# Attention, MoE and gated MoE on one core: batches 1 to 3 of the first MoE as four blocks of 432 tokens, single q and k rows, one ring of three decode tiles

## The chip, the core and the metric

The kernel runs on 1 core of a Trainium2 chip. The time is that of the device in microseconds (us). Before the change it is 1085.62 us, the median of 3 runs (1084.67 to 1086.32). One further execution was profiled; all rows below are from it.

## The reference, cut to what matters

```python
# q, k, v: 4 batches, 8 heads, 576 tokens, 64 wide
local = softmax(causal(q @ k.T / 8)) @ v
mem   = (phi(q) @ M_prev) / (phi(q) @ z_prev + 1e-6)     # phi(x) = elu(x) + 1
attn  = g * mem + (1 - g) * local                        # g = sigmoid(beta), one per head
x = attn as [2304 tokens, 512]
h = x @ w_in                 # 512 -> 2048    the first MoE
x = (h * sigmoid(h)) @ w_out # 2048 -> 512
g, val = x @ w_gate, x @ w_val   # 512 -> 1536   the second MoE
out = (g * sigmoid(g) * val) @ w_out2            # 1536 -> 512
```

All weights and inputs come as 64-bit floats. q, k and v are read as they are handed over to the kernel in 32 bits; the MoE weights arrive as 64-bit words, and the kernel decodes them to 32 bits on chip.

## The kernel before

A matmul of the MoEs is done in three passes of fp32r, as a 32-bit number is split into a high part (rounded to fp32r) and a low part: high times high, low weight times high x, high weight times low x. That is why a product over 512 inputs (4 tiles of 128) takes 12 matmuls.

Attention is done in units. A unit is a batch and a pair of heads (128 rows). Batch 0 has two units for a pair: phase A for its first 256 tokens, phase B for the other 320. Batches 1 to 3 (phase G) have one unit for all 576. A unit loads rows of q, k and v, transposes q and k on TensorE (L340), makes the scores (L407, L482), their exponentials on ScalarE, scales them (L496 on GpSimd, L500 on ScalarE), transposes them, multiplies by v (`AV`, L592), and `put_x` (L306) writes the result, 128 of the 512 inputs of the MoE, as a high part (ScalarE, L314) and a low part (VectorE, L315). The four pairs of a batch together fill its x. Rows of q, k and v stand in two sets of tiles used in turn (`rows`, L228); `nxt_load` (L604) loads the rows of the unit after the next, q and k in the stage `lq`, v in `lv`.

The first MoE (`moe1`, L799) is a list of segments. A segment is a block of tokens and a slice of 512 of the 2048 hidden numbers: 4 hidden tiles of 12 matmuls each (`s1`, L829: "h"), and then 4 output tiles of 12 matmuls each (L888: "y"), 96 matmuls in all. For each hidden tile ScalarE makes the tanh (L836), VectorE the product (L837), ScalarE the high part gh (L838), and GpSimd the low part gl (L839). Output tiles are added up over the slices in yp (L891 on ScalarE for the first slice, L893 on VectorE), and written to DRAM after the last. Each batch has two blocks, of 256 and of 320 tokens, hence 8 segments a batch, 32 in all. The first two hidden tiles of a segment are issued before the output tiles of the one before (`la`). A slice needs 8 tiles of split weights of 512 KB; they are decoded and split once, written to DRAM, and read back (w<-wd, L733) whenever the slice comes again.

The second MoE's weights are decoded and split beside all this by `prep_w2` (L930): 36 tiles, each loaded as raw 64-bit words (L690, L695; the load waits for a one-column copy on GpSimd, L688), decoded by one ScalarE instruction (L704) and three on VectorE (L705 to L707) into a tile t from a ring of 4, combined in sums on GpSimd (L976 to L979, L1002 to L1005), split (high on ScalarE, low on GpSimd, L956), and written to DRAM (L941). It is advanced by one step after every third group of 12 matmuls while attention goes on (`every`), and after every third group once attention is done (`late`, L1068). After the last segment the second MoE runs on TensorE in an order written out by hand (L1164, L1271).

How far attention is at each segment is set by `goals` (L1369 on): a batch's attention is to be done when the cost (matmul columns) of the segments before its first one has been issued, less a share. A scheduler then settles the order on each engine by its own model of time, and SyncE issues all these DMAs in one queue, in order.

## Time and profile before

| | us |
|---|---|
| median of 3 runs | 1085.62 |
| the profiled execution's own time | 1084.78 |
| its span, first to last instruction | 1083.0 |
| TensorE busy in matmuls | 1048.6 (97%) |
| VectorE, ScalarE, GpSimd busy | 704.4, 547.7, 405.6 |
| last "y" of the first MoE ends at | 679.4 |

A row of a window gives, for a stretch of the span, the busy time of each engine and in brackets its number of instructions. A row of the timeline gives the start, the time to the end of the last of its instructions, the engine, the line, the operation, the tiles and "x" with the count. Matmuls of one row overlap, so the spacing of matmuls is read from the starts of two rows, not from the duration of one.

### The profile page before, as it was taken

The page shows a single profiled execution, that of the slowest core. Times are in us where ns is not written, and L with a number is a line of the kernel's source. Part 1 is how long each engine was busy: PE and PEld are TensorE (multiplying, and loading weights), DVE is VectorE, ACT ScalarE, POOL GpSimd, SP SyncE. Part 2 cuts the span into 40 slices and gives each one's busy share as a digit, 9 for nine tenths or more (in the row PEclk, how much of TensorE's full clock was granted, in tenths as well). Part 3 has the DMA queues.
Part 4 walks back from the last instruction along what each step waited for, and adds up shares of the span by engine and source line. Part 5 has one row for each costly group of instructions (what it writes and reads, how often), then busy time and mean ns, then how long its engine had stood idle before and what let it go on. Part 6 is the DMA issues. An engine that isn't in the chain of part 4 may idle for free.

```text
span 1083.0 us, 20683 instructions
## 1 busy us (share of the span) xinstructions
PE 1048.6 (97%) x7390; PEld 977.9 (90%) x7390; DVE 704.4 (65%) x1633; ACT 547.7 (51%) x1319; POOL 405.6 (37%) x493
## 2 busy tenths in 40 slices
PE   7788999999999999999999999999999999999998
PEld 5566888888999898989889999999999999999998
DVE  7897588987566665456766654465854569355573
ACT  6655586766557565646655543233622336232351
POOL 4577445568566563757543985000000000000000
PEclk9889999999999999999999999999999999999999
DMA  7968576566688664975628899777887778877784
GB/s 180 299 206 259 144 245 198 171 189 208 207 263 252 207 191 128 313 258 187 209 69 303 318 365 311 258 251 247 329 293 231 262 253 277 280 241 247 258 278 151
DMA packets 169831, 258.29 MB, mean 238 GB/s; under 512 B 76928, under 2 KB 114304, under 8 KB 169728
## 3 DMA queue, kind: packets, MB, share of 16 engines
q1 hardware_dynamic: 168640, 256.70, 71.8%
q8 instruction: 59, 0.97, 0.4%
q10 hardware_dynamic: 1088, 0.26, 0.1%
q14 instruction: 44, 0.36, 0.1%
HBM read 197.67 MB, written 59.24 MB: 237 GB/s over the span
## 4 chain that ended last, share of the span: by engine, by line
PE 76%; DVE 8%; DMA 7%; POOL 4%; issue 2%; ACT 1%; SPq 1%; POOLq 0%; DVEq 0%; ACTq 0%
PE h L829 14%; PE y L888 13%; PE oac L1164 10%; PE gb L1164 10%; PE po L1271 9%; PE pb L1271 4%; PE gd L1164 3%; PE U L592 3%; PE pst L340 3%; PE pss L407 3%; DMA raw<-in_moe_w_gate_dram 2%; DMA raw<-in_moe_w_val_dram 1%; PE psm L418 1%; PE pss L482 1%; POOL s L496 1%
## 5 line engine op out<-in xcount | busy, mean ns | idle before, releaser
L888 PE MATMUL y<-gh,w 128*128 128x320 f32 (+1 forms) x1024 | 172.8, 305 | 3.7 <-DVE yp L893 1.3
L829 PE MATMUL h<-xh,w 128*128 128x320 f32 (+1 forms) x1024 | 171.8, 305 | 4.2 <-DVE th L837 2.0
L829 PEld LDWEIGHTS h<-xh,w 128*128 128x128 f32 x1024 | 145.3, 190 | 13.7 <-issue 5.0
L888 PEld LDWEIGHTS y<-gh,w 128*128 128x128 f32 x1024 | 146.2, 190 | 9.2 <-DVE th L837 2.1
L839 POOL TENSOR_TENSOR gl<-th,gh 128x256 fp32r<-128x256 f32 (+1 forms) x128 | 113.1, 886 | 99.3 <-ACT gh L213 83.8
L1164 PE MATMUL gb<-yT,w 128*128 128x384 f32 x648 | 124.8, 336 | 0.0
L1164 PEld LDWEIGHTS gb<-yT,w 128*128 128x128 f32 x648 | 113.1, 188 | 0.0
L837 DVE SCALAR_TENSOR_TENSOR th<-th,h 128x256 f32<-128x256 f32 (+1 forms) x128 | 57.3, 449 | 73.8 <-ACT th L836 73.7
L888 PE MATMUL y<-gl,w 128*128 128x320 f32 (+1 forms) x512 | 94.4, 300 | 0.1
L1271 PE MATMUL po<-w,ph 128*128 128x256 f32 x516 | 93.8, 283 | 0.0
L829 PE MATMUL h<-xl,w 128*128 128x320 f32 (+1 forms) x512 | 91.8, 299 | 0.0
L496 POOL TENSOR_TENSOR s<-s,r 128x128 f32<-128x128 f32 (+4 forms) x96 | 72.5, 781 | 48.5 <-DVE r L508 14.0
L463 ACT ACTIVATE s<-s,mn 128x128 f32<-128x128 f32 (+3 forms) x128 | 71.0, 556 | 35.8 <-DVE mn L459 34.5
L1164 PE MATMUL oac<-yB,w 128*128 128x384 f32 x432 | 81.3, 336 | 0.0
L1271 PEld LDWEIGHTS po<-w,ph 128*128 128x128 f32 x516 | 81.2, 191 | 0.0
L1236 ACT CAST ph<-r 128x384 fp32r<-128x384 f32 x108 | 51.0, 513 | 55.7 <-DVE r L1190 35.7
L213 ACT CAST gh<-th 128x256 fp32r<-128x256 f32 (+1 forms) x128 | 55.0, 432 | 45.5 <-DVE th L837 39.6
L888 PEld LDWEIGHTS y<-gl,w 128*128 128x128 f32 x512 | 76.7, 190 | 1.2 <-issue 0.7
L829 PEld LDWEIGHTS h<-xl,w 128*128 128x128 f32 x512 | 75.9, 190 | 0.9 <-issue 0.4
L1164 PEld LDWEIGHTS oac<-yB,w 128*128 128x128 f32 x432 | 75.4, 188 | 0.0
L1271 PE MATMUL po<-w,pl 128*128 128x256 f32 x258 | 73.0, 283 | 0.0
L340 PE MATMUL pst<-ident,s 128*128 128x128 f32 x400 | 60.7, 279 | 10.2 <-POOL s L496 4.7
(166 smaller groups left out, 2152.2 us busy)
## 6 DMA issues: line engine op xcount, KB each, us to landing
w<-wg SPq DMA_DIRECT2D x108, 512.0 KB, 4.7
w<-wd SPq DMA_DIRECT2D x80, 512.0 KB, 5.5
wg<-wo SPq DMA_DIRECT2D x36, 512.0 KB, 3.5
w<-woT SPq DMA_DIRECT2D x36, 512.0 KB, 4.9
wd<-w SPq DMA_DIRECT2D x32, 512.0 KB, 3.3
raw<-in_moe_w_out_dram SPq DMA_DIRECT2D x28, 512.0 KB, 5.7
w<-woB SPq DMA_DIRECT2D x27, 512.0 KB, 4.7
w<-wg SPq DMA_DIRECT2D x36, 256.0 KB, 4.8
```

Source lines behind the costliest of these rows:

```text
L213: nc.scalar.copy(out, in_)
L340: nc.tensor.matmul(dst, src, ident[0:n, 0:n], start=start, stop=True, is_transpose=True, skip_group_check=True)
L407: lambda m=m, qx=qx, kx=kx, hh=hh, r=slice(64 * hh, 64 * hh + 64): nc.tensor.matmul(dst(hh), o[qx][r, x:x + P], o[kx][r, 0:w], start=(m == ...
L463: nc.scalar.activation(out=a, in_=a, func=ACTF.Exp, scale=-1.0, bias=mn, accum_out=o["sm", sup][:, col:col + 1])
L496: nc.gpsimd.tensor_mul(a, a, r.to_broadcast([P, w]))
L829: nc.tensor.matmul(ps[:, :nt], w[:, kk, :], x[:, kk, :nt], start=(m == 0), stop=(m == 3 * KD - 1))
L837: nc.vector.scalar_tensor_tensor(th[:, :nt], th[:, :nt], 1.0, ps[:, :nt], ALU.add, ALU.mult)
L839: tt(CFG["gl" if n >= CFG["n0"] else "gl0"]).tensor_sub(gl[:, :nt], th[:, :nt], f(gh[:, :nt]))
L888: nc.tensor.matmul(ps[:, :nt], w[:, c], g[:, :nt], start=(m == 0), stop=(m == last))
L1164: nc.tensor.matmul(dst, w[wi][:, P * kk:P * kk + P], y[ny][:, yi, kk], start=(start and m == 0), stop=(stop and m == 5), skip_group_check= ...
L1236: nc.scalar.copy(ph, src)
L1271: nc.tensor.matmul(dst, a[:, c], x, start=(begin and m == 0 and own_bank), stop=(end and m == 2), skip_group_check=True,)
```

## The change

Batch 0 keeps its blocks of 256 and 320. The 1728 tokens of batches 1 to 3 become four blocks of 432 (called t0 to t3 here), which run across the borders of batches: t0 holds tokens of batch 1 only, t1 of batches 1 and 2, t2 of 2 and 3, t3 of 3. t0 goes through its four slices alone, then t1 alone, then t2 and t3 together slice by slice. So the first MoE has 8 + 16 = 24 segments. `put_x` writes a unit's tokens into one or two blocks. x and yp get new homes: x of batch 0 and then of t2 in one tile, those of t0 and t3 in another, that of t1 in a third, which is later yp of t3.

q and k rows exist once; the rows for the next unit (no longer the one after it) are loaded in `lq`, after this unit's transposes. v keeps two tiles.

`decode` takes its tile from one ring of three for the weights of both MoEs; before, the first MoE's weights had a ring of 2 and those of the second one of 4.

`late` becomes 0.75: once attention is done, `prep_w2` is advanced after three of four groups of matmuls.

```diff
-    raw=2,
-    yp=2,
+    raw=3,
...
-    late=3,
+    late=0.75,
...
-    TM = SB
+    TB = 432
+    NB1 = (B - 1) * S // TB
+    TM = max(SB, TB)
...
-            t = {nm: ld.tile([P, 5, 2, D], F32, name=f"{nm}_t{i}") for nm in "qkv"}
+            t = dict(rows[0]) if i else {nm: ld.tile([P, 5, 2, D], F32, name=f"{nm}_t{i}") for nm in "qk"}
+            t["v"] = ld.tile([P, 5, 2, D], F32, name=f"v_t{i}")
...
     def put_x(b, p, sup, U, E):
         n = (SA, SB)[sup]
...
+        if b == 0:
+            todo = [(("b", sup), 0, 0, n)]
+        else:
+            g0, todo = (b - 1) * S + (0, SA)[sup], []
+            x0 = g0
+            while x0 < g0 + n:
+                x1 = min(g0 + n, (x0 // TB + 1) * TB)
+                todo.append((("t", x0 // TB), x0 % TB, x0 - g0, x1 - g0))
+                x0 = x1
+        for key, at, c0, c1 in todo:
+            xh, xl = x_tile(key)
+            d = slice(at, at + c1 - c0)
+            n_x[key] = n_x.get(key, 0) + c1 - c0
+            cp(E("xhi"), xh[:, p, d], U[:, c0:c1])
+            nc.vector.tensor_sub(xl[:, p, d], U[:, c0:c1], f(xh[:, p, d]))
...
-            w = u + len(rows)
+            w = u + (len(rows) if names == "v" else 1)
...
+    order = [(("b", "AB".index(x[0])), int(x[1])) for x in CFG["order"].split()]
+    for blks in [(0,), (1,), tuple(range(2, NB1))]:
+        for s in [order[-1][1]] + [x for x in range(NSL) if x != order[-1][1]]:
+            order += [(("t", i), s) for i in blks]
...
-            t = decode(raw, cur["pw"].tile([P, 512], F32, tag="t", name="t2", bufs=CFG["pt"]))
+            t = decode(raw)
...
-            if n % CFG["late"] == 0:
+            if int(n * CFG["late"]) > int((n - 1) * CFG["late"]):
```

Three places show how the instructions move. The first is TensorE where attention ends: the last unit's product with v (U), and the "h" and "y" matmuls around it. Before:

```order
L888 MATMUL y<-gl,w 128x320 x2
L592 MATMUL U<-tb,v_t_104 64x192 x2
L592 MATMUL U<-ta,v_t_104 64x256
L592 MATMUL U<-tb,v_t_104 64x64 x2
L592 MATMUL U<-tb,v_t_104 64x320 x6
L592 MATMUL U<-ta,v_t_104 64x256
L592 MATMUL U<-ta,v_t_104 64x128 x2
L888 MATMUL y<-gl,w 128x320
L829 MATMUL h<-xh,w 128x256 x5
L829 MATMUL h<-xl,w 128x256 x3
```

The same place in the changed kernel (L619 is the product with v, L871 "h", L929 "y"):

```order
L367 MATMUL U<-ident,mr_6406 128x128 x2
L871 MATMUL h<-x,w 128x432 x3
L619 MATMUL U<-tb,v_t_102 64x192 x2
L619 MATMUL U<-ta,v_t_102 64x256 x2
L619 MATMUL U<-ta,v_t_102 64x128 x2
L619 MATMUL U<-tb,v_t_102 64x64 x2
L619 MATMUL U<-tb,v_t_102 64x320 x6
L871 MATMUL h<-x,w 128x432 x39
L929 MATMUL y<-gh,w 128x432 x4
```

The matmuls have 432 columns in place of 256 and 320, and no "y" stands between U and the first block that needs all of it.

The second is GpSimd after the last attention: gl is the low part that "y" waits for, S, wo and raw are steps of `prep_w2`. Before:

```order
L1005 TENSOR_TENSOR S_8470<-t_8406,S_8470 128x256
L839 TENSOR_TENSOR gl<-th,gh 128x320
L956 TENSOR_TENSOR wo<-t_8406,wo 128x2x256
L956 TENSOR_TENSOR wo<-S_8470,wo 128x2x256
L839 TENSOR_TENSOR gl<-th,gh 128x320
L956 TENSOR_TENSOR wo<-S_8470,wo 128x2x256
L1002 TENSOR_TENSOR S_8722<-t_8598 128x256
L839 TENSOR_TENSOR gl<-th,gh 128x320 x2
```

Now:

```order
L881 TENSOR_TENSOR gl<-th,gh 128x432 x2
L997 TENSOR_TENSOR wo<-S_7247,wo 128x2x256
L715 COPY raw_7468<-gl 128x1
L1043 TENSOR_TENSOR S_7403<-raw 128x256
L1045 TENSOR_TENSOR S_7403<-raw 128x256
L1044 TENSOR_TENSOR S_7403<-raw,S_7403 128x256
L997 TENSOR_TENSOR wo<-raw,wo 128x256
L1046 TENSOR_TENSOR S_7403<-raw,S_7403 128x256
L997 TENSOR_TENSOR wo<-raw,wo 128x256
L715 COPY raw_7508<-gl 128x1
L881 TENSOR_TENSOR gl<-th,gh 128x432
```

Between one gl and the next there stand nine instructions of `prep_w2` in the rows now, and one to two in those of before. In all, behind the last attention scaling GpSimd now has 32 gl of 432 columns, 21 one-column copies, 44 sums, 32 splits of 512 and 11 of 256 columns; before it had 35 gl, 11 copies, 23 sums, 18 and 5 splits there.

The third is SyncE's queue in batch 0's second phase, with the rows of q and k (q_t, k_t), the raw weights (raw), and the split weights on their way to DRAM (wd). Before, with the loads for the first two units of that phase already far ahead:

```order
L770 DMA wd_3_317<-w 128x1024
L295 DMA q_t_98<-in_q_dram 128x2x64 x2
L722 DMA raw_430<-in_moe_w_out_dram 128x4x256
L302 DMA q_t_98<-in_q_dram 128x2x64
L295 DMA k_t_99<-in_k_dram 128x2x64 x2
L302 DMA k_t_99<-in_k_dram 128x2x64
L690 DMA raw_646<-in_moe_w_in_dram 128x4x256
L770 DMA wd_4_373<-w 128x1024
```

Now, where these are the loads for the second unit:

```order
L797 DMA wd_3_309<-w 128x1024
L749 DMA raw_422<-in_moe_w_out_dram 128x4x256
L297 DMA q_t_98<-in_q_dram 128x2x64 x2
L304 DMA q_t_98<-in_q_dram 128x2x64
L797 DMA wd_4_365<-w 128x1024
L297 DMA k_t_99<-in_k_dram 128x2x64 x2
L304 DMA k_t_99<-in_k_dram 128x2x64
L797 DMA wd_5_421<-w 128x1024
```

The rows of k now stand behind the fifth split weight tile, and they are wanted one unit earlier. From the second MoE's first matmul on, the rows of TensorE are the same in both kernels.

## Rows read from the trace of the kernel before

**Rows 1.** The page: busy time, share, instructions.
```profile
PE 1048.6 (97%) x7390; PEld 977.9 (90%) x7390; DVE 704.4 (65%) x1633; ACT 547.7 (51%) x1319; POOL 405.6 (37%) x493
```
**Rows 2.** Windows: busy PE, PEld, DVE, ACT, POOL (count), clock, DMA share, GB/s.
```profile
0.00:100.00 100.00, 84.11 (x468) 58.14 (x468) 84.94 (x236) 64.53 (x172) 60.47 (x75) 0.91 0.79 233
100.00:272.00 172.00, 165.76 (x1240) 145.63 (x1241) 135.55 (x362) 116.64 (x303) 102.38 (x115) 1.00 0.63 196
272.00:405.00 133.00, 131.48 (x1018) 122.24 (x1016) 81.45 (x217) 79.75 (x205) 77.61 (x101) 1.00 0.70 225
405.00:575.00 170.00, 164.43 (x1259) 150.69 (x1257) 99.69 (x265) 97.50 (x246) 94.87 (x121) 1.00 0.59 197
575.00:680.00 105.00, 103.44 (x761) 102.33 (x762) 60.32 (x100) 46.97 (x106) 70.28 (x82) 1.00 0.90 319
680.00:1083.00 403.00, 399.40 (x2651) 398.88 (x2649) 242.49 (x457) 142.34 (x293) 0.00 (x0) 1.00 0.76 259
```
**Rows 3.** Timeline of TensorE: runs of 256, 320 and 384 columns.
```profile
656.45 1.12 PE L829 MATMUL h<-xh,w 128*128 128x256 f32 x8
657.41 0.64 PE L829 MATMUL h<-xl,w 128*128 128x256 f32 x4
...
659.33 1.34 PE L829 MATMUL h<-xh,w 128*128 128x320 f32 x8
660.50 0.75 PE L829 MATMUL h<-xl,w 128*128 128x320 f32 x4
661.09 1.34 PE L829 MATMUL h<-xh,w 128*128 128x320 f32 x8
...
1020.94 2.24 PE L1164 MATMUL gb<-yT,w 128*128 128x384 f32 x12
1023.02 2.24 PE L1164 MATMUL oac<-yB,w 128*128 128x384 f32 x12
```
**Rows 4.** GpSimd's groups from 575 to 680 us: count, busy us, mean ns.
```profile
L839 POOL TENSOR_TENSOR gl<-th,gh 128x320 fp32r<-128x320 f32 x16 | 16.0, 1008 | 9.5 <-ACT gh L213 4.8 <-PE y L888 4.7
L839 POOL TENSOR_TENSOR gl<-th,gh 128x256 fp32r<-128x256 f32 x16 | 13.6, 847 | 19.2 <-ACT gh L213 13.7 <-PE y L888 3.1 <-PE h L829 2.4
L956 POOL TENSOR_TENSOR wo<-S,wo 128x512 fp32r<-128x512 f32 x10 | 13.4, 1343 | 0.0
...
L956 POOL TENSOR_TENSOR wo<-t,wo 128x256 fp32r<-128x256 f32 x5 | 4.6, 920 | 0.0
...
L1002 POOL TENSOR_TENSOR S<-t 128x256 f32<-128x256 f32 x5 | 3.9, 780 | 2.5 <-DVE t L707 2.3
...
L688 POOL COPY raw<-gl 128x1 f32<-128x1 f32 x10 | 2.7, 285 | 0.2
```
**Rows 5.** Two windows inside the last stage of the first MoE.
```profile
600.00:650.00 50.00, 48.84 (x367) 48.64 (x366) 27.08 (x46) 23.65 (x55) 45.95 (x53) 1.00 0.98 354
605.00:620.00 15.00, 13.84 (x106) 13.64 (x105) 9.14 (x14) 6.97 (x17) 14.88 (x17) 1.00 0.97 355
```
**Rows 6.** Waits up to 280 us: us in total, times, longest.
```profile
ACT raw L704 <- POOL w L747: 3.6, 5, 1.3
```
**Rows 7.** DMA issues, 30 to 60 us: count, KB each, median us to landing.
```profile
k_t<-in_k_dram SPq DMA_DIRECT2D x7, 64.0 KB, 4.3
```
**Rows 8.** Timeline of TensorE: k transposes of batch 0's units five and six.
```profile
36.61 0.49 PE L340 MATMUL psk<-ident,k_t 128*128 128x128 f32 x3
45.29 0.55 PE L340 MATMUL psk<-ident,k_t 128*128 128x128 f32 x3 [1.11 <-DVE mn L459]
```
**Rows 9.** Timeline of TensorE behind the last unit's U.
```profile
567.55 0.42 PE L888 MATMUL y<-gl,w 128*128 128x320 f32 x1
568.08 0.86 PE L829 MATMUL h<-xh,w 128*128 128x256 f32 x5
```
**Rows 10.** The page's DMA issues: split weights read back.
```profile
w<-wd SPq DMA_DIRECT2D x80, 512.0 KB, 5.5
```
**Rows 11.** SyncE's waits: us in total, times, longest.
```profile
SPq L941 <- POOL wo L956: 97.0, 53, 11.2
```

More of the change, by code (lines that the diff above doesn't have):

```diff
@@ L289, in load_rows @@
         for nm in names:
-            owner[nm, u % len(rows)] = u
+            owner[nm, u % len(rows) if nm == "v" else 0] = u
             src = {"q": q, "k": k, "v": v}[nm]
@@ L304, with x_tile @@
     xs, mx2, n_x, keep = {}, [], {}, {}
+    def x_tile(key):
+        if key not in xs:
+            if key[0] == "b":
+                n, (x0, words) = (SA, SB)[key[1]], ((0, 2 * KD * SA), (2 * KD * SA, 2 * KD * S))[key[1]]
+                if "x0" not in xs:
+                    xs["x0"] = mx.tile([P, 2 * KD * S], F32R, tag="x", name="x", bufs=1)
+                t = xs["x0"][:, x0:words]
+            else:
+                n = TB
+                if key[1] == 2:
+                    t = mx.tile([P, 2 * KD * S], F32R, tag="x", name="x", bufs=1)[:, 0:2 * KD * TB]
+                else:
+                    t = mx2[0].tile([P, 2 * KD * TB], F32R, tag=f"x{key[1] % 3}", name="x", bufs=1)
+            t = t.rearrange("p (w k n) -> p w k n", w=2, k=KD)
+            xs[key] = t[:, 0], t[:, 1]
+        return xs[key]
     def put_x(b, p, sup, U, E):
         n = (SA, SB)[sup]
[L308 to L315 removed]
+        if b == 0:
+            todo = [(("b", sup), 0, 0, n)]
+        else:
+            g0, todo = (b - 1) * S + (0, SA)[sup], []
[10 more added lines that the diff above has]
+            nc.vector.tensor_sub(xl[:, p, d], U[:, c0:c1], f(xh[:, p, d]))
     BLK = ((0, 1), (2, 3, 4))
@@ L332, in own @@
         def own(nm):
-            assert ph == "A" or owner[nm, u % len(rows)] == u, (nm, u)
+            assert ph == "A" or owner[nm, u % len(rows) if nm == "v" else 0] == u, (nm, u)
         def row_of(nm, c):
@@ L669, in load_B @@
         for u in range(NP, NP + len(rows)):
-            load_rows(u, "qkv")
+            load_rows(u, "qkv" if u == NP else "v")
     slots[1].insert(0, setup_beta)
@@ L701, in decode @@
         if t is None:
-            t = cur["raw"].tile([P, 512], F32, tag="raw", name="raw")
+            t = cur["raw"].tile([P, 512], F32, tag="raw", name="raw", bufs=CFG["raw"])
         ti = t.bitcast(I32)
@@ L780, with token_block, new_yp @@
     prep1 = Prep(raw_w1, split_w1)
-    A0, B0 = (0, SA), (SA, SB)
-    order = [(0, (A0, B0)["AB".index(x[0])], int(x[1])) for x in CFG["order"].split()]
-    for b in range(1, B):
-        sl = [order[-1][2]] + [x for x in range(NSL) if x != order[-1][2]]
-        blks = [A0, B0]
-        for i, s in enumerate(sl):
-            order += [(b, blk, s) for blk in (blks if i % 2 == 0 or CFG["blks"] else blks[::-1])]
+    def token_block(key):
+        kind, i = key
+        if kind == "b":
+            return dict(key=key, t0=(0, SA)[i], nt=(SA, SB)[i], r=ready[0, i])
+        return dict(key=key, t0=S + TB * i, nt=TB, r=ready[1 + (TB * (i + 1) - 1) // S, 1])
+    order = [(("b", "AB".index(x[0])), int(x[1])) for x in CFG["order"].split()]
+    for blks in [(0,), (1,), tuple(range(2, NB1))]:
+        for s in [order[-1][1]] + [x for x in range(NSL) if x != order[-1][1]]:
+            order += [(("t", i), s) for i in blks]
     segs = []
-    for n, (b, blk, s) in enumerate(order):
-        same = [x[2] for x in order if x[:2] == (b, blk)]
+    for n, (key, s) in enumerate(order):
+        same = [x[1] for x in order if x[0] == key]
         segs.append(dict(
-            b=b, blk=blk, s=s, first=same[0] == s, last=same[-1] == s,
-            last_use=n + 1 < len(order) and order[n + 1][2] != s,
+            token_block(key), s=s, first=same[0] == s, last=same[-1] == s,
+            last_use=n + 1 < len(order) and order[n + 1][1] != s,
         ))
     yps = {}
+    def new_yp(key):
+        kind, i = key
+        if kind == "t" and i == 3:
+            t = f(mx2[0].tile([P, 2 * KD * TB], F32R, tag="x1", name="x", bufs=1))
+            return t[:, 0:KD * TB].rearrange("p (k n) -> p k n", k=KD)
+        if key == ("b", 1):
+            t = yps["both"]
+        else:
+            t = yps["both"] = mx.tile([P, KD * S], F32, tag="yp", name="yp", bufs=1)
+        x0, n = {("b", 0): (0, SA), ("b", 1): (KD * SA, SB)}.get(key, (0, TB))
+        return t[:, x0:x0 + KD * n].rearrange("p (k n) -> p k n", k=KD)
     def moe1():
@@ L1370 @@
         for sg in segs:
[L1371 removed]
+            r = sg["r"]
             if not goals or r > goals[-1][1]:
```

30 lines of the change are left out of this document (10 added, 20 removed).

## The prediction

> **What bounds the kernel now.** I read the page's engine shares first: TensorE is busy 97% of the span, VectorE 65%, ScalarE 51%, GpSimd 37% [rows 1]. A share is an average, so I went to the windows by stage [rows 2]. The reader is to see there that TensorE idles 15.9 us in the first 100 us, 6.2 in the next 172, 1.5 in the 133 us after that, 5.6 in the 170 us in which attention ends, 1.6 in the 105 us in which the first MoE runs beside the second one's weight preparation, and 3.6 in the second MoE. The granted clock is 1.00 from 100 us on, which is 2.4 GHz. From 100 us on TensorE is therefore the bound, and what counts is how long it takes to issue its matmuls. The second MoE (from 680 us) is untouched, as its order on TensorE stays the same.
>
> A busy TensorE is not one at its best rate, so the third view is the timeline, for the spacing of matmuls [rows 3]. With 256 columns, 8 matmuls take from 656.45 to 657.41, 120 ns each. With 320, 12 take from 659.33 to 661.09, 146.7 ns. With 384, 12 take from 1020.94 to 1023.02, 173.3 ns. 64 more columns cost 26.7 ns both times, which is one column per cycle at 2.4 GHz. What is left is the same for all three: 120 - 106.7 = 13.3 ns for each matmul, whatever its width.
>
> **Fewer, wider matmuls.** Batches 1 to 3 have 24 segments of 96 matmuls, half of them 256 and half 320 columns wide: 1152 x 120 + 1152 x 146.7 ns = 307.2 us. Now they have 16 segments of 96 with 432 columns. 432 is 48 more than 384, so 173.3 + 48/2.4 = 193.3 ns, an estimate by the slope of [rows 3]: 1536 x 193.3 ns = 296.9 us. The columns are the same (663,552 in both), so the difference of 10.3 us is 768 matmuls less, at 13.3 ns. All of it lies on TensorE's path. The step in width beyond 384 is small, so I give it only 0.2 us either way.
>
> The Trainium skill (TensorE: Matmul & The Clock Gate, section Back-to-back issue gap) has a warm, isolated spacing of N/2.4 + 2.5 ns. By that rule 768 matmuls less would save 1.9 us only, which no measurement of this kernel tells from nothing. The trace does not agree with it here: 13.3 ns in three widths, where each matmul also loads its weights. The measurement decides, and the rule stays as a rival with a small chance.
>
> **Attention beside fewer matmuls.** The attention of batches 2 and 3 lay beside 2 x 102.4 us of matmuls of the first MoE (307.2/3 a batch) and now has t0 and t1 beside it, 2 x 74.2 us (296.9/4 each). The stretch from 272 to 575 us shrinks by 56.3 to about 247 us. In it VectorE worked 181.1 and ScalarE 177.2 of 303 us [rows 2]. If all of that work stayed, VectorE would be at 73% and ScalarE at 72%; some goes, as there are fewer segments and fewer preparation steps. The stretch from 100 to 272 us shows a denser case: VectorE 79%, ScalarE 68%, and TensorE idles 3.6%. So TensorE's idle time here, 7.1 us of 303 (2.3%) before, becomes between 2.3% and 3.6% of 247, 5.8 to 8.9 us: a change of -1.3 to +1.8. I take +0.5, a little past the middle, since attention is nearer to the dense case and without the first MoE's decoding.
>
> **The last stage: preparation moves there.** With `late` at 0.75, 21 of the 36 raw tiles are fetched behind the last attention scaling (11 before). By the counts of the order and GpSimd's durations [rows 4]: gl of 432 columns is 1008 + 112 x (1008 - 847)/64 = 1290 ns; 32 x 1.29 + 21 x 0.285 + 44 sums x 0.78 + 32 x 1.343 + 11 x 0.92 = 134.7 us. TensorE has 8 segments there, 96 x 8 x 193.3 ns = 148.5 us. So GpSimd must be busy 91% of it, where it was 67% from 575 to 680 us [rows 2]. DMA was at 0.98 of its engines when the preparation was busiest, at 354 GB/s [rows 5]. I add up 21 raw tiles (11 MB), splits to DRAM (20), three slices of weights (12.6), the next stage's first weights and y (6) and yd (2): 51 MB in 148.5 us, 343 GB/s, so the same load now lasts the whole stage. What that costs is in [rows 5] too: at 92% GpSimd from 600 to 650 us TensorE idled 1.16 of 50 us (2.3%), all of it from 605 to 620 us, where GpSimd was busy 14.88 of 15 us (TensorE 7.7% idle). For 148.5 us against 1.6 us idle before: at the old stage's own rate (1.5%) 2.2 us, +0.6; at 2.3% 3.4 us, +1.8; at 7.7% 11.4 us, +9.8. I take +1.8, as 91% is the load of the 50 us.
>
> **Single q and k rows.** k transposes of units five and six stand at 36.6 and 45.3 us [rows 8]. A load takes 4.3 us to land [rows 7], so after 37.1 it could be there at 41.4, 3.9 us early; but in the queue it stands behind the fifth split weight tile, which waits for GpSimd. I put 0 to +3 us on it for this one unit, late by that much at most; in batches 2 and 3 eight units share 247 us, 31 us each, and the load is issued in the third of a unit's eight slots, so it has some 19 us. TensorE idles there anyway, 15.9 us in the first 100, so +0.5. On the other side the ring of three: ScalarE waited 3.6 us in 5 waits for the old ring's tile to be freed by GpSimd [rows 6]. It is idle a third of that stretch, so I count 0, with -3.6 as the bound. For the second MoE the ring shrinks from 4 to 3; a tile is now reused as early as three steps later (four groups of 12 x 193.3 ns, 9.3 us), and with GpSimd at 91% that is part of the cost above.
>
> **At no cost.** `put_x` gets one piece more in 12 units: 12 copies and 12 subtractions of about half a us on engines that TensorE does not wait for in most of the stretch. At the end of attention TensorE stood 0.4 us between the one "y" behind U (567.55, 147 ns) and "h" (568.08) for the last x [rows 9]. Now no "y" stands there, but three "h" matmuls of the first pairs of heads do, 0.58 us. It costs nothing, or 0.4 us. Weight slices of t0 and t1 come every 18.6 us of matmuls (25.6 before) plus attention. A weight tile of a slice is issued after its predecessor's last use and wanted some 16 us later (one "h", four "y", two "h" tiles of 2.3 us), and lands in 5.5 us [rows 10].
>
> **Sum.** -10.3 + 0.5 + 1.8 + 0.5 = -7.5 us. The profiled execution took 1084.78 us, so its like would take 1077.3; the median lies 0.8 above it, so I predict 1078.1.
>
> **Rivals.**
> 1. GpSimd becomes the bound of the last stage (slower). Place: gl in GpSimd's queue behind up to nine preparation steps, and SyncE's queue, where weight loads stand behind splits that wait for GpSimd, 97 us in 53 waits, up to 11.2 us [rows 11]. If TensorE idles throughout as it did from 605 to 620 us, the stage costs +9.8, and +1.8 with attention at its dense end, +3 from the early load: 1085.6 - 10.3 + 14.6 = 1089.9. It decides where the stage takes 9.3 us more than at the old idle (10.3 less the two 0.5), that is where GpSimd reaches less than 85% of its time (134.7 of 148.5 + 1.6 + 9.3 us). For it: 91% is wanted for 150 us, and over the whole old stage it was 67% [rows 2]. Against it: when it was pressed, it ran at 92 to 99% [rows 5], and the groups of 432 leave more time between two gl. Chance 0.14.
> 2. The gain is eaten, no change. Either a wider matmul saves much less than 13.3 ns: if one of 432 columns took 198.8 ns, 1536 of them would take 305.3 us, 1.9 less than before, and with the 2.8 us of the other terms the time is 1086.5. (This is the saving that the rule of 2.5 ns in the Trainium skill, cited above, would give.) Or attention's chain of steps, not any engine's sum, is too long for 74 us of matmuls a batch: at an idle rate of 6% of 247 us in t0 and t1, 15 us against 7.1, the sum is -10.3 + 8 + 2.3 = 0 and the time 1085.6. For it: the first 100 us idle 16%. Against it: those 100 us are the start, where little else can run; the densest stretch after them idles 3.6% [rows 2]; and [rows 3] has the same 13.3 ns three times. Chance 0.10.
> 3. More is gained: the ring of three takes the 3.6 us away, attention idles at 2.3%, and the last stage at its old rate: -10.3 - 1.3 + 0.6 - 3.6 = -14.6, 1071. Everything would have to fall well. Chance 0.06.
>
> **How the numbers follow.** The forecast has 0.70, with its own range 1073 to 1083. The whole range reaches up to 1088, into the first rival, and down to 1071: 1071 to 1088. A difference of 0.2% (2.2 us) is what a measurement of this kernel can tell. Faster by more has 0.70 + 0.06, less a little of the forecast's upper edge, so 0.75; the same has the second rival and that edge, 0.11; slower has 0.14.
>
> **What the profile would show.** Right: "h" and "y" rows of 432 columns with starts 193 ns apart; 6622 matmuls in place of 7390; the last "y" near 672 us (679.4 before); GpSimd about 90% busy in the last stage and TensorE idle there by 2 to 4 us. Wrong: TensorE rows with long idle times that end with gl, with a weight's DMA or with yp in the last 150 us of the first MoE; TensorE idle over 4% in t0 and t1, ended by VectorE or ScalarE; or a spacing at 432 columns away from 193 ns.

## The result: slower by 1.3%, and the profile after

| | before | after |
|---|---|---|
| median, us | 1085.14 (4 runs beside it) | 1099.76 (1097.40 to 1101.89, 4 runs) |
| ratio | | 1.0133, interval 1.0110 to 1.0156 |
| span of the profiled execution, us | 1083.0 | 1100.1 |
| matmuls | 7390 | 6622 |
| batch 0's last "y" ends, us | 271.7 | 276.4 |
| last product with v (U) ends, us | 567.6 | 517.8 |
| last "y" of the first MoE ends, us | 679.4 | 680.6 |
| from there to the end of the span, us | 403.6 | 419.5 |

The prediction was 1078.1 us, faster: wrong in sign and outside its range. In the rows below PE is TensorE, PEld its weight loads, DVE VectorE, ACT ScalarE, POOL GpSimd and SPq SyncE's queue. The page's busy line of the kernel after answers to [rows 1]:

```profile
PE 1054.4 (96%) x6622; PEld 964.0 (88%) x6622; DVE 711.3 (65%) x1589; ACT 541.6 (49%) x1259; POOL 409.9 (37%) x461
```

There are 768 matmuls fewer, as the change says, and yet TensorE is busy longer (1048.6 before). So something other than idle time was added. The windows of the kernel after, with the columns of [rows 2], show what:

```profile
0.00:100.00 100.00, 83.50 (x442) 56.83 (x444) 83.09 (x238) 63.63 (x170) 61.33 (x76) 0.86 0.79 234
100.00:272.00 172.00, 167.06 (x1244) 146.96 (x1241) 133.83 (x360) 117.55 (x304) 98.09 (x110) 0.99 0.62 193
272.00:515.00 243.00, 241.27 (x1501) 210.90 (x1501) 138.45 (x401) 142.44 (x348) 112.83 (x135) 1.00 0.60 195
515.00:683.00 168.00, 157.14 (x787) 144.86 (x785) 112.14 (x133) 74.87 (x145) 136.38 (x139) 0.98 0.83 287
683.00:700.00 17.00, 8.79 (x27) 7.96 (x28) 2.00 (x4) 1.57 (x4) 1.28 (x1) 0.60 0.78 275
700.00:1100.00 400.00, 396.67 (x2628) 396.47 (x2627) 241.83 (x456) 141.50 (x291) 0.00 (x0) 0.99 0.75 253
```

Attention beside the wide blocks (272 to 515 us) is nearly seamless: 1.7 us idle of 243. The last stage idles 10.9 us in 168, 2.4 of them already behind the last "y". And from 683 to 700 us, where the second MoE begins, TensorE works 8.8 of 17 us, at a mean granted clock of 0.60. The clock, 1.00 from 100 us on in [rows 2], is now below that in several windows.

The waits of the stretch from 515 to 700 us in the kernel after (us in total, times, longest):

```profile
ACT raw L731 <- POOL wo L997: 22.1, 9, 4.8
ACT e L1243 <- DMA woT<-wo: 10.5, 1, 10.5
PE oac L1205 <- ACT e L1243: 7.2, 1, 7.2
PE y L929 <- DVE th L879: 4.4, 1, 4.4
PE oac L1205 <- DVE x L934: 2.9, 1, 2.9
```

The timeline of all engines at the border, kernel after (the last two splits of the preparation, their DMAs on SyncE, the last "y", and the second MoE's first matmuls):

```profile
679.08 1.52 PE L929 MATMUL y<-gl,w 128*128 128x432 f32 x7
680.81 1.26 POOL L997 TENSOR_TENSOR wo<-S,wo 128x512 fp32r<-128x512 f32 x1 [1.14 <-ACT wo L214]
682.10 0.80 SPq L982 DMA_DIRECT2D woT<-wo  x2
683.46 2.29 PE L1205 MATMUL oac<-yB,w 128*128 128x384 f32 x6 [2.86 <-DVE x L934]
684.31 1.28 POOL L997 TENSOR_TENSOR wo<-S,wo 128x512 fp32r<-128x512 f32 x1 [2.24 <-ACT wo L214]
686.57 2.23 SPq L1187 DMA_DIRECT2D w<-wg  x2
688.90 0.85 SPq L982 DMA_DIRECT2D woT<-wo  x2
690.18 0.33 PE L1216 MATMUL gd<-yB,w 128*128 128x384 f32 x1
697.13 0.48 ACT L1243 COPY e<-oac 128x384 f32<-128x384 f32 x1 [10.52 <-DMA woT<-wo]
697.66 4.21 PE L1205 MATMUL oac<-yB,w 128*128 128x384 f32 x12 [7.15 <-ACT e L1243]
```

This is read backwards. The matmuls at 697.66 waited for ScalarE's copy `e`. `e` waited 10.5 us for the write of a split weight tile, because its memory is that which the preparation had used (`open_2` closes the pools of `prep_w2` and opens its own). That write was issued at 688.90, behind weight loads in SyncE's queue, as GpSimd had made the split only at 684.31 to 685.6, five us after the last "y". Twelve matmuls of 384 columns then take 4.21 us, and 2.24 in [rows 3]: the clock was at its lower level, 1.2 GHz. That `e` waits for its memory is read from the program and the trace; no run gave `e` other memory.

The wait ahead of it, 2.86 us up to 683.46, is another chain. On VectorE the last output tiles are added up (x, L934) behind an addition for y (ytop, L1088), which waited for rows of y from DRAM. In ring4 and late1 that wait of TensorE is 0.6 us:

```profile
681.66 1.23 DVE L1088 TENSOR_TENSOR ytop<-ybot,ytop 128x768 f32<-128x768 f32 x1 [1.19 <-DMA ybot<-yd]
682.81 1.62 DVE L934 SCALAR_TENSOR_TENSOR x<-y,x 128x432 f32<-128x432 f32 x3
```

In the kernel before, the last split of the preparation ended at 669.07, 10.4 us before the last "y":

```profile
666.51 2.56 POOL L956 TENSOR_TENSOR wo<-S,wo 128x512 fp32r<-128x512 f32 x2
```

### The profile page after: what moved, and what is told of

Its sections match the earlier page's. It is cut to its first block, busy times and chain, and to the rows that moved or that the text cites. A ratio compares the mean times of both kernels' runs of the same rounds, so it can differ in the third digit from the quotient of the medians.

```text
span 1100.1 us, 18920 instructions
## 1 busy us (share of the span) xinstructions
PE 1054.4 (96%) x6622; PEld 964.0 (88%) x6622; DVE 711.3 (65%) x1589; ACT 541.6 (49%) x1259; POOL 409.9 (37%) x461
## 4 chain that ended last, share of the span: by engine, by line
PE 68%; DVE 10%; DMA 7%; POOL 6%; issue 5%; ACT 2%; SPq 2%; POOLq 0%; ACTq 0%; DVEq 0%
PE oac L1205 10%; PE gb L1205 10%; PE y L929 10%; PE h L871 9%; PE po L1312 8%; PE pb L1312 4%; PE gd L1205 3%; PE pss L434 3%; PE U L619 3%; PE pst L367 3%; DVE raw L733 2%; POOL wo L997 2%; DVE raw L734 2%; DMA woT<-wo 2%; POOL gl L881 2%
## 5 line engine op out<-in xcount | busy, mean ns | idle before, releaser
L871 PE MATMUL h<-x,w 128*128 128x432 f32 (+2 forms) x1152 | 227.1, 347 | 1.9 <-ACT x L214 0.9
L871 PEld LDWEIGHTS h<-x,w 128*128 128x128 f32 x1152 | 198.0, 192 | 14.7 <-issue 3.8
L929 PE MATMUL y<-gh,w 128*128 128x432 f32 (+2 forms) x768 | 169.0, 351 | 6.6 <-DVE th L879 4.4
L929 PEld LDWEIGHTS y<-gh,w 128*128 128x128 f32 x768 | 132.3, 191 | 19.3 <-ACT gh L214 4.8
L881 POOL TENSOR_TENSOR gl<-th,gh 128x432 fp32r<-128x432 f32 (+2 forms) x96 | 106.9, 1116 | 86.7 <-ACT gh L214 70.0
L929 PE MATMUL y<-gl,w 128*128 128x432 f32 (+2 forms) x384 | 89.0, 346 | 2.3 <-POOL gl L881 2.3
L879 DVE SCALAR_TENSOR_TENSOR th<-th,h 128x432 f32<-128x432 f32 (+2 forms) x96 | 52.4, 548 | 55.3 <-ACT th L878 55.1
L732 DVE TENSOR_SCALAR raw<-raw 128x512 int32<-128x512 int32 x68 | 46.1, 678 | 49.5 <-ACT raw L731 46.8
L731 ACT ACTIVATE raw<-raw 128x512 f32<-128x512 f32 x68 | 45.7, 672 | 55.4 <-POOL wo L997 22.1
L929 PEld LDWEIGHTS y<-gl,w 128*128 128x128 f32 x384 | 67.3, 189 | 6.3 <-POOL gl L881 3.5
L214 ACT CAST gh<-th 128x432 fp32r<-128x432 f32 (+2 forms) x96 | 49.0, 512 | 46.6 <-DVE th L879 43.0
L486 DVE CUSTOM_DVE_ANT_0 s<-pss,mask 128x128 f32<-128x128 f32 (+3 forms) x128 | 58.5, 484 | 16.9 <-PE pss L434 16.7
```

The costliest lines, as they stand in the source:

```text
L214: nc.scalar.copy(out, in_)
L486: nc.vector.tensor_tensor_reduce(out=a, in0=at[i](hh), in1=mask[:, 512 - w:512], op0=ALU.add, op1=ALU.min, scale=1.0, scalar=3.0e38, accum ...
L732: nc.vector.tensor_single_scalar(ti, ti, 3, op=ALU.logical_shift_left)
L871: nc.tensor.matmul(ps[:, :nt], w[:, kk, :], x[:, kk, :nt], start=(m == 0), stop=(m == 3 * KD - 1))
L879: nc.vector.scalar_tensor_tensor(th[:, :nt], th[:, :nt], 1.0, ps[:, :nt], ALU.add, ALU.mult)
L881: tt(CFG["gl" if n >= CFG["n0"] else "gl0"]).tensor_sub(gl[:, :nt], th[:, :nt], f(gh[:, :nt]))
```

## The experiments

Three theories stood at the start. R: the ring of three delays decoding by itself. G: GpSimd has too much preparation in the last stage. B: the border waits because the preparation ends too late. For the runs with blocks of 432 two numbers are compared. The hole is what the second MoE's start costs: span, less the end of the last "y", less 403.6 us, which is that rest in the kernel before. Beside it stands by how much GpSimd's last instruction ends after the last "y" (minus: before it; -4.6 before and about -6.3 with 432 columns is the last gl, with no preparation behind it). Idle is TensorE's, summed from the trace, from batch 0's last "y" to U and from U to the last "y". All but the medians and the ratios are of one profiled execution; U stands at a somewhat different place in the first MoE in each, so "U to y" is not quite the same work.

| kernel | median us | ratio to before (interval) | idle to U | idle U to y | U to y | GpSimd's end | hole |
|---|---|---|---|---|---|---|---|
| before | 1085 | 1 | 6.0 | 2.7 | 111.8 | -4.6 | 0 |
| after | 1099.8 | 1.0133 (1.0110 to 1.0156) | 1.7 | 8.5 | 162.8 | +5.0 | 15.9 |
| after_again | 1100.2 | 1.0146 (1.0123 to 1.0168) | 3.2 | 7.6 | 162.0 | +5.3 | 13.7 |
| fill | 1096.3 | 1.0121 (1.0094 to 1.0148) | 1.6 | 7.8 | 162.2 | +5.2 | 13.5 |
| ring4 | 1090.2 | 1.0039 (1.0020 to 1.0058) | 1.8 | 8.5 | 161.7 | +2.0 | 7.7 |
| late1 | 1087.6 | 1.0024 (1.0009 to 1.0039) | 1.9 | 9.2 | 164.1 | -1.9 | 1.3 |
| late1_yp | 1105.1 | 1.0186 (1.0162 to 1.0210) | 2.9 | 11.6 | 166.4 | +4.3 | 14.6 |
| every2 | 1080.5 | 0.9966 (0.9929 to 1.0003) | 3.5 | 5.9 | 159.5 | -6.4 | 0.0 |
| both | 1082.1 | 0.9981 (0.9964 to 0.9999) | 2.4 | 8.7 | 163.7 | -6.4 | 0.3 |
| both_yp | 1078.9 | 0.9943 (0.9919 to 0.9967) | 2.4 | 5.1 | 157.7 | -6.3 | 0.0 |
| all_four | 1080.3 | 0.9963 (0.9947 to 0.9980) | 2.7 | 6.5 | 160.1 | -6.2 | 0.4 |
| every1_ring4 | 1093.9 | 1.0094 (1.0072 to 1.0116) | 14.6 | 0.0 | 156.2 | -6.4 | 0.0 |
| every1_yp | 1093.6 | 1.0083 (1.0057 to 1.0109) | 13.0 | 0.0 | 156.2 | -6.4 | 0.0 |

**ring4**, a fourth decode tile:

```diff
-    raw=3,
+    raw=4,
```

> The changed kernel with one edit: the decode ring has four tiles in place of three. Theory R (the ring of three): in the last stage ScalarE's decode (L731) stood 22.1 us in 9 waits until GpSimd had split the tile decoded three steps earlier, and tanh, gh and the splits' high parts stood behind it in ScalarE's queue. With a fourth tile those waits fall under 5 us, the preparation ends some 12 us earlier, and the time falls from 1099.8 to 1088 or less. Theory G (GpSimd has too much work: 136 of 168 us in the last stage): the sums and splits are the same, so the waits only move to another place in the chain and the time stays within 3 us, 1097 to 1101. Theory B (only the border to the second MoE is late, whatever made the preparation late): says nothing by itself; the time must move with the end of the preparation, one for one.

Measured: 1090.2 us, 9.5 less, short of theory R's 1088. ScalarE's decode waits for GpSimd's split 5.9 us in 2 waits in place of 22.1 in 9, and the preparation ends 3.0 us earlier against the last "y", not 12. The ring of three delays the preparation; but the last stage is as long as in the changed kernel, and the hole is 8.2 us smaller (6.0 against after_again), so most of what the fourth tile gave came at the border. It does not come one for one: from late1 to the two profiles of the changed kernel, GpSimd's end moves by some 7 us and the hole by 12 to 15.

**every2**, a preparation step after every second group of matmuls while attention goes on (third before):

```diff
-    every=3,
+    every=2,
```

> The changed kernel with one edit: while attention goes on, the weight preparation is advanced at every second group of matmuls in place of every third. 13 of the 72 steps, about 6.5 tiles or 29 us of GpSimd's work, move from the last stage into t0 and t1, where GpSimd was busy 113 of 243 us and TensorE idle under 1%. Theory G: the last stage keeps about 107 of 136 us on GpSimd, the preparation ends before the last output tile, the 15 us between the first MoE's last matmul and the second MoE's steady run go, and the stage loses little: 1078 to 1083 us. Theory R: the ring's waits move along with the work into the attention stage, where ScalarE and VectorE are fuller; the border is repaired but 5 us and more are lost in t0 and t1: 1084 to 1090. If neither the border nor the stage moves, both are wrong.

Measured: 1080.5 us, 19 less, with the ring still at three. No hole is left. Too much of the preparation had been left for the last stage, as theories G and B have it; this run does not tell the two apart.

**before_ring3** and **before_late**: the kernel before with the shared ring of three alone, and with `late` at 0.75 alone.

```diff
-    raw=2,
+    raw=3,
...
-            t = cur["raw"].tile([P, 512], F32, tag="raw", name="raw")
+            t = cur["raw"].tile([P, 512], F32, tag="raw", name="raw", bufs=CFG["raw"])
...
-            t = decode(raw, cur["pw"].tile([P, 512], F32, tag="t", name="t2", bufs=CFG["pt"]))
+            t = decode(raw)
```

```diff
-    late=3,
+    late=0.75,
```

> The kernel before with one part of the change: both MoEs' decoded tiles come from one ring of three (before: rings of two and of four). Blocks, rows and the preparation's rate stay. Theory R: ScalarE's decode waits for GpSimd here too, above all from 590 to 665 us where GpSimd is busy 78%; the time rises by 4 us or more, to 1089 to 1095. Theory G: the old last stage has slack (GpSimd 67% busy), so the time stays within 2 us of 1085.1.

> The kernel before with one part of the change: once attention is done the weight preparation is advanced at three of four groups of matmuls in place of one of three. The 11 raw tiles left at that point are then pressed into about half of the last stage. Theory G: GpSimd's work there is 83 us of 102 and its order only shifts to the front; TensorE may lose some us while GpSimd is full and the border becomes free earlier: 1083 to 1088. Theory R: the old ring of four is enough, same forecast, so this run tells apart only whether the faster rate alone costs TensorE time (over 1090) or not.

Measured: 1087.8 us (ratio 1.0007 to 1.0043) and 1086.6 us (1.0003 to 1.0027), 3 and 2 us slower; the first lies between the two forecasts, the second is as expected. Neither makes a hole there: in both, GpSimd's last instruction, a gl, ends 4.7 us before the last "y". Where the preparation is not late, these parts cost some us; what takes them was not followed up.

**both**, ring4 and every2 together:

> The changed kernel with a fourth decode tile and a preparation step after every second group while attention goes on. Theory R (the ring of three stalls ScalarE by itself, wherever the preparation lies): its 9.5 us come on top of what every second group gave, 1080.5 - 9.5 = 1071 us. Theories G and B (GpSimd has too much preparation in the last stage, and it ends too late for the second MoE): with less work left there, a tile comes free in time anyway, and the fourth tile is worth 3 us at most: 1077 to 1081 us, border without a hole in both kernels. What both theories leave is VectorE's burst of preparing y for the second MoE near 545 to 555 us, with a wait of TensorE of 3 to 4 us and a granted clock of 0.5 behind it.

Measured: 1082.1 us, not different from every2, and far from theory R's 1071. The fourth tile, worth 9.5 us where the preparation ends late, is worth nothing where it ends in time. Theory R is refuted as a cost of its own.

**late1**, a preparation step after every group once attention is done:

```diff
-    late=0.75,
+    late=1,
```

> The changed kernel with a preparation step after every group once attention is done, in place of three of four. The work of the last stage stays the same; it is only asked for earlier. Theory B (what costs is the end: the last split, its write and the memory that e needs at the border): the hole of 15.8 us at the border shrinks to under 6, and the time is 1087 to 1091 us. Theory G (GpSimd can't do this work in the stage at all): what the border gives back the stage loses, the last y comes at 686 to 692 in place of 680.6, and the time is 1096 to 1101 us.

Measured: 1087.6 us. This moves none of the work out of the last stage, it only asks for it earlier; the stage is 1.2 us longer, the hole all but gone, and 12 us of the 14.6 are back. So it was the time at which the preparation ends, not its amount in the stage, that made most of the loss. Theory B is shown.

**both_yp** and **late1_yp**: VectorE's preparation of y for the second MoE held behind the last product th, on both and on late1.

```diff
-            nc.vector.scalar_tensor_tensor(th[:, :nt], th[:, :nt], 1.0, ps[:, :nt], ALU.add, ALU.mult)
+            cur["th"] = nc.vector.scalar_tensor_tensor(th[:, :nt], th[:, :nt], 1.0, ps[:, :nt], ALU.add, ALU.mult)
...
-                next(y, None)
+                with tc.issue_after(cur["th"].ins):
+                    next(y, None)
```

It was made because of these rows of VectorE in the kernel after: the last four of six instructions for y in a row, ahead of the th for which TensorE waits until 554.80.

```profile
547.62 1.49 DVE L1075 TENSOR_TENSOR yB<-ybot,yB 128x768 fp32r<-128x768 f32 x1
549.03 1.87 DVE L1075 TENSOR_TENSOR yT<-ytop,yT 128x768 fp32r<-128x768 f32 x1
550.83 1.47 DVE L1075 TENSOR_TENSOR yB<-ybot,yB 128x768 fp32r<-128x768 f32 x1
552.22 2.01 DVE L1092 TENSOR_TENSOR yt<-ybot,ytop 128x768 f32<-128x768 f32 x1
554.16 0.59 DVE L879 SCALAR_TENSOR_TENSOR th<-th,h 128x432 f32<-128x432 f32 x1
```

TensorE in the same place, kernel after, and the window around it:

```profile
549.07 1.34 PE L929 MATMUL y<-gh,w 128*128 128x432 f32 x6
554.80 2.61 PE L929 MATMUL y<-gh,w 128*128 128x432 f32 x6 [4.40 <-DVE th L879]
...
550.00:560.00 10.00, 5.60 (x17) 4.59 (x16) 9.96 (x9) 4.82 (x9) 10.00 (x8) 0.66 0.49 170
```

Six matmuls take 2.61 us behind the wait and 1.34 before it: the clock has fallen to its lower level, and the window's mean is 0.66. (In ring4 the same burst took 0.96 us an instruction, and TensorE waited 4.6 us all the same, for gh.)

> As the kernel with both, but VectorE may take each step that prepares y for the second MoE only behind the last product th issued before that step (a different order of VectorE's instructions, the same work). Theory Y (the burst of nine instructions of 1 to 2 us ahead of a th starves TensorE once, and the clock falls to its lower level for some microseconds): 5 to 7 us less than the kernel with both, no clock of 0.5 between the last U and the last y. Rival, GpSimd's queue is what limits the last stage: within 1.5 us of it, the wait only moves to gl.

> The changed kernel with a preparation step after every group once attention is done, and VectorE's preparation of y held behind the last product th. Theory Y (the burst on VectorE is a stall of its own, also where GpSimd is dense): 3 to 5 us less than the 1087.6 us without the hold, 1083 to 1085 us, no granted clock of 0.5 near 553 us. Rival G (GpSimd's queue limits the stage, the burst only shows first): 1086 to 1089 us, the wait moves to gh or gl, 8 us or more idle behind the last U.

Measured: on both, 3.2 us less where 5 to 7 were expected, and the two intervals just overlap. The wait for th is gone, but not the low clock that theory Y ruled out: TensorE now waits 3.1 us for gh, and the next matmuls are slow again (from 560 to 570 us the mean granted clock is 0.85).

```profile
567.32 2.17 PE L929 MATMUL y<-gh,w 128*128 128x432 f32 x5 [3.09 <-ACT gh L214]
```

The profiled execution of both is 6 us above its median and that of both_yp 5 below, so their spans are not compared. On late1 it is 17.5 us more. There the wait for th and the fall of the clock at 553 us are gone too, but the preparation ends late again, and the hole is back. Two rows of the waits of late1_yp, 515 to 700 us, show a new one in ScalarE's queue, in which decoding stands:

```profile
ACT yT L1074 <- DVE ytop L1088: 5.6, 1, 5.6
PE oac L1206 <- ACT e L1244: 6.9, 1, 6.9
```

That this wait alone moved the preparation's end is argued, not shown. Both forecasts missed the time. Of the rival's signs, those of the stage came: the wait moved to gh and gl (8.3 and 3.2 us), with 11.6 us idle behind the last U. The burst is not a cause that can be removed by itself.

**all_four**, both_yp with `late` at 1:

> The changed kernel with a fourth decode tile, a preparation step after every second group while attention goes on and after every group behind it, and VectorE's preparation of y held behind the last product th. If the causes are the border and the burst (B and Y), nothing is left that the last step could give, since the preparation ends in time already: 1077 to 1080 us, as without the change of late. If the preparation's pace still delays something at the border: 1073 to 1076 us.

Measured: 1080.3 us, not different from both_yp. Where the preparation ends in time, its pace gives nothing more.

**every1_ring4** and **every1_yp**, `every` at 1 with four decode tiles, without and with the hold on VectorE:

> The changed kernel with a fourth decode tile and a preparation step after every group while attention goes on, so that little of the preparation is left for the last stage. Theory G (the density of GpSimd's work made the last stage long): the stretch from the last U to the last y falls from 160 to 164 us to 152 to 155 us, and if attention does not pay for it the time is 1073 to 1077 us. Theory Y: the burst on VectorE is still there, one wait of 3 to 5 us near 550 us with a clock of 0.5 behind it, the stretch is 157 to 160 us and the time 1079 to 1083 us. A third way: attention's stretch pays what the last stage gains, TensorE idle there by 6 us or more, 1080 to 1085 us.

> The same, with VectorE's preparation of y held behind the last product th. By G nothing changes against the kernel without the hold (within 2 us); by Y the wait near 550 us and the low clock behind it go, and it is 4 to 6 us faster.

Measured: 1093.9 and 1093.6 us. The third way came, further than expected. Windows of every1_ring4, attention's part and the last stage:

```profile
272.00:515.00 243.00, 233.56 (x1407) 199.73 (x1403) 190.87 (x432) 159.19 (x385) 191.47 (x222) 0.99 0.85 292
528.00:684.00 156.00, 156.00 (x797) 149.16 (x796) 48.34 (x72) 44.59 (x80) 36.69 (x32) 1.00 0.39 128
```

With GpSimd at 24% (36.69 of 156 us) the last stage has no idle time, a clock of 1.00, and the hold makes no difference: its stalls were those of a dense preparation (theory G, for the stage's own 8 us). That it is GpSimd's share of it is not shown, as VectorE's work and the DMA share fell as well; and the stage is 156.2 us, not 152 to 155. But with GpSimd and VectorE at 79% beside attention, TensorE idles 9.4 us there in place of 1.7. The median is 11.8 us above that of both; the 12.2 us more that TensorE idles ahead of U are its largest part seen, and the rest was not taken apart.

**before_qk1**, the kernel before with single q and k rows alone:

```diff
-            t = {nm: ld.tile([P, 5, 2, D], F32, name=f"{nm}_t{i}") for nm in "qkv"}
+            t = dict(rows[0]) if i else {nm: ld.tile([P, 5, 2, D], F32, name=f"{nm}_t{i}") for nm in "qk"}
+            t["v"] = ld.tile([P, 5, 2, D], F32, name=f"v_t{i}")
...
-            w = u + len(rows)
+            w = u + (len(rows) if names == "v" else 1)
...
```

> The kernel before with single rows of q and k, nothing else. By the prediction this costs 0.5 us (0 to 3): 1085 to 1088 us, batch 0 ends its y at 271.7 to 275. Rival: half of the 4.7 us by which batch 0 ends later in the changed kernel, and TensorE's idle time in the later batches, come from it: 1088 to 1091 us.

Measured: 1081.5 us, ratio 0.9958 to 0.9982: 3.3 us faster, below both expectations. Its first window, beside 0.91 of [rows 2]:

```profile
0.00:100.00 100.00, 78.99 (x474) 54.74 (x475) 88.33 (x248) 64.66 (x172) 63.59 (x77) 0.97 0.82 240
```

By this sum the clock accounts for it: span times one less the mean granted clock, the time by which TensorE's clock fell short, has a median over the executions of 4.3 us here and 8.7 in the kernel before, and the times less that are 1077.2 and 1076.0. Why the clock falls less here is not shown.

**fill** and **after_again**: the wait for `e` filled with 35 repeated matmuls, beside the changed kernel as it is.

```diff
-                nc.tensor.matmul(
-                    t[:, :HT], r_(w[:, 0])[:, 0:P], y["B11"][:, 0, 0], start=True, stop=True, skip_group_check=True
-                )
+                for _ in range(36 if (i, j, tag) == (0, 0, "d") else 1):
+                    nc.tensor.matmul(
+                        t[:, :HT], r_(w[:, 0])[:, 0:P], y["B11"][:, 0, 0], start=True, stop=True, skip_group_check=True
+                    )
```

> The changed kernel with one matmul of the second MoE's beginning (the one that fills gd, 384 columns) issued 36 times over in place of once, the same result each time; it stands where TensorE waited 7.15 us for the copy e, so that the wait is filled with 35 x 0.173 = 6.1 us of matmuls. Theory C (what a wait costs is the wait and then some 7 us at a granted clock of 0.5): the second fall of the clock at the border is gone, and although 35 matmuls are added the time is 3 us less than that of the changed kernel, 1096 to 1097 us. Rival (the wait alone costs): the same time as the changed kernel, 1099 to 1101 us.

> The changed kernel as it is, in the same call, to compare the others with: 1098 to 1101 us. By theory C its executions differ by what the clock takes: time without it (the time less the span times one less the mean granted clock) near 1079 us.

Measured: 1096.3 and 1100.2 us, but the intervals of the ratios overlap, and the holes of the two profiles are the same (13.5 and 13.7). The time is inconclusive. The timelines are not: fill first, then after_again.

```profile
684.22 6.41 PE L1217 MATMUL gd<-yB,w 128*128 128x384 f32 x36
691.45 2.36 PE L1205 MATMUL oac<-yB,w 128*128 128x384 f32 x12 [0.81 <-ACT e L1244]
```

```profile
685.73 0.34 PE L1216 MATMUL gd<-yB,w 128*128 128x384 f32 x1
691.52 4.18 PE L1205 MATMUL oac<-yB,w 128*128 128x384 f32 x12 [5.45 <-ACT e L1243]
```

Where TensorE was kept at work, the twelve matmuls behind the wait take 2.36 us, and the mean granted clock from the first gd on is 1.00 (684.5 to 695 us); where it stood 5.45 us, they take 4.18, and it is 0.67 (686 to 696.5 us). Here a wait is paid once as a wait and again in the matmuls behind it. That the hole is the same in spite of it has a reason in these two profiles: the matmuls behind `e` start 17.2 us behind the last "y" in fill and 15.6 in after_again, and that takes back the 1.8 us. Whether filling a wait makes the kernel faster stays open.

**widths**, 24 matmuls each of ten widths on the tiles of the first MoE, added to both_yp, one execution:

```diff
             ps = bank("h")
+            if n == 18 and j == 2:
+                for nn in (256, 320, 352, 384, 400, 408, 416, 424, 428, 432):
+                    for m in range(24):
+                        nc.tensor.matmul(
+                            ps[:, :nn], (wh, wl)[m // 4 % 2][:, m % KD, :], xh[:, m % KD, :nn], start=True, stop=True
+                        )
```

> The kernel both_yp with 240 matmuls added on TensorE in the last stage of the first MoE, ahead of the third hidden tile of the eleventh segment of batches 1 to 3: 24 each with 256, 320, 352, 384, 400, 408, 416, 424, 428 and 432 columns of the same x and the same weights, a weight load each, into the tile h, which the proper matmuls overwrite afterwards. Theory W (a width past some point costs more than a cycle a column): 120, 146.7, 160 and 173.3 ns for the first four, as in the kernel before, and from some width on 3 ns more than columns/2.4 + 13.3, up to 196.6 at 432. Theory M (the new tiles' place costs 3 ns whatever the width): 123, 150, 163 and 176.6 ns for the first four. In sum 240 matmuls, some 41 us more than without them.

It was made because of rows like this one in the timeline of the kernel after, in which 48 matmuls start at 606.06 and the next row at 615.49: 196.5 ns each, where 193.3 were forecast.

```profile
606.06 9.59 PE L871 MATMUL h<-x,w 128*128 128x432 f32 x48
615.49 1.92 PE L929 MATMUL y<-gh,w 128*128 128x432 f32 x9
```

Measured (mean from start to start, from the first of a width to the first of the next; some 2 ns of it are scatter, as 424 and 428 columns show):

| columns | 256 | 320 | 352 | 384 | 400 | 408 | 416 | 424 | 428 | 432 |
|---|---|---|---|---|---|---|---|---|---|---|
| ns | 118.2 | 147.2 | 161.5 | 175.2 | 181.8 | 186.2 | 190.2 | 194.1 | 193.6 | 196.2 |
| less columns/2.4 | 11.6 | 13.9 | 14.8 | 15.2 | 15.1 | 16.2 | 16.9 | 17.5 | 15.2 | 16.2 |

Neither theory: there is no clear step, and no constant extra. From 256 to 432 columns a matmul costs 78.0 ns more, 0.44 ns a column and not 0.417. The 384 columns of [rows 3] were of the second MoE, and their 173.3 ns made the line look straighter than it is on these tiles. The other engines' work is not the reason: in the quiet last stage of every1_ring4, 48 matmuls of 432 columns take from 613.53 to 622.95 us, 196.3 ns each. What makes the wide ones dearer was not found.

```profile
613.53 9.59 PE L871 MATMUL h<-x,w 128*128 128x432 f32 x48
622.95 2.31 PE L929 MATMUL y<-gh,w 128*128 128x432 f32 x11
```

## Why the prediction was wrong, step by step

- **Fewer, wider matmuls (-10.3):** halved. 1536 x 196.5 ns = 301.8 us against 307.2 is -5.4 us. What failed is "193.3 ns, an estimate by the slope", with 0.2 us either way. The rule that was weighed there, which the Trainium skill (TensorE: Matmul & The Clock Gate, section Back-to-back issue gap) gives for isolated matmuls, N/2.4 + 2.5 ns, does not hold for this stream either: widths shows 11.6 to 17.5 ns beside the columns.
- **Attention beside fewer matmuls (+0.5):** better than its range. TensorE's idle time from batch 0's end to U is 1.7 and 3.2 us in two profiles of the changed kernel against 6.0, though U stands elsewhere in the first MoE.
- **The last stage (+1.8):** the step that failed. It had the facts (21 raw tiles left, GpSimd wanted 91% of the time) and priced them by the idle time inside the stage. That is +5.8 and +4.9 us in two profiles, inside the bound of +9.8. GpSimd's work was counted well, 134.7 us against 136.4 in the window from 515 to 683 us, but the stage grew, so that is 81% of it. And the main cost is behind the stage, where no term stood: the preparation ends 5 us after the last "y", and the second MoE's start waits for it, 13.7 to 15.9 us with the low clock. In the kernel before the preparation ended 10.4 us before the last "y"; the prediction did not work out when it would end.
- **Ring of three (0):** it was priced from the old ring's waits in the first 280 us, 3.6 us [rows 6], and its smaller size for the second MoE was put under the +1.8. There, in the last stage, ScalarE waits 22.1 us for GpSimd, where the ring of four of the kernel before has no such wait. The fourth tile is worth 9.5 us where the preparation is late (ring4) and nothing where it is not (both against every2).
- **Single q and k rows (+0.5):** wrong in sign where tried alone, -3.3 us; without the clock's share it would be +1.2, inside the 0 to 3.
- **The clock:** "1.00 from 100 us on" was taken over from the kernel before, and no term had it. The time by which the clock fell short has a median of 9.7 us over 17 executions of the kernel before and 23.6 over 6 of the changed one measured beside them (after_again); the times less that are 1075.1 and 1077.5. Part of it falls into idle time, where it costs nothing, and part of it follows from the waits themselves.

From batch 0's end to the end of the span the changed kernel takes 12.4 us (first profile) and 13.5 us (second) more than the kernel before. Up to the last "y" it takes 3.5 and 0.2 us less, where the forecast had 8 less for that part; from there on it takes the 15.9 and 13.7 us of the hole more. So the border is the main part of the miss. Of what is lacking ahead of it, the width is 4.9 us; the clock falls short by 3.4 and 6.8 us there, in part in idle time; and idle time grew by 1.5 and 2.2 us in all, about the +2.3 that two terms had. This adds up to 3 to 4 us more than was measured, which was not taken apart; attention work that moves across the end of batch 0 may be in it. Before that point the two profiles differ by 8 us between themselves (276.4 and 268.4), so the start tells nothing of the change.

Rival 1 had the right side and resource, and its mark came (GpSimd at less than 85% of the stage), but not its place and price: the main wait is not for gl, it is the second MoE's, for the last split's write, and the time is 10 us above its 1089.9.

The best version run is both_yp, 1078.9 us, 0.9919 to 0.9967 of the kernel before: the change does pay, 6 us, with its three edits (a fourth decode tile, `every` at 2, the hold on VectorE). How much of that the blocks of 432 give is not shown, as single q and k rows alone gave the kernel before 3.3 us.

## What to carry to other kernels

Where a change makes one stage shorter, whatever was paced by that stage is left over: work out not only if the next stage has room for it, but when it now ends, and who waits for its end (its memory, too). In these traces a wait of some microseconds on TensorE was paid twice, once as a wait and once in a lower clock, so a sum of idle times was too small. A cost per instruction read at three sizes, from two stages, is a thin line to extend to a fourth size.

## What the runs showed of the hardware

- The granted clock fell to its lower level, 1.2 GHz, at each of the seven waits of 2.9 to 7.2 us that TensorE has past 100 us in the two profiles of the changed kernel, and matmuls behind them took up to twice their time: 2.61 us for six after a wait of 4.40 us, 1.34 us before it; 4.21 us for twelve after 7.15 us, 2.24 in [rows 3]. With 35 matmuls in place of such a wait (fill) it did not fall there. It fell without such a wait as well: at 266 us in the first profile, where TensorE was busy 8.6 of the 10.3 us ahead of it.
- Executions of one kernel differ by it where it falls often: over the 12 executions of both, the span grows by 0.73 us for each us by which the clock fell short (correlation 0.83), over the 12 of all_four by 0.68 (0.76). For the kernel before it is not shown: four sets of 11 to 30 executions give 0.06 to 0.74 (correlation 0.04 to 0.62).
- VectorE and GpSimd were slow beside each other, now the one, now the other. In the kernel after, the last four instructions of VectorE's burst on 768 columns took 1.5 to 2.0 us each, with GpSimd busy all the time. In ring4 the burst ran at 0.96 us an instruction, and the one sum that GpSimd made beside it (L1017) took 3.54 us, where it took 0.74 at 546.14 us in the kernel after. What decides which of the two is slow was not tried.
